# Loading wq by two issues of 16 and 112 partitions in a one-core decode kernel

## The chip, the cores and the metric

The kernel runs on one core of a Trainium2 chip. The metric is the time of one execution on the device, in microseconds; a kernel's time is the median of its runs. The core has five engines that run side by side, each with its own list of instructions: TensorE (PE in the profile; PEld are its weight loads), VectorE (DVE), ScalarE (ACT), GpSimd (POOL) and SyncE (SP), which here does nothing but issue transfers. Transfers between the device's main memory and the core's on-chip memory are carried by 16 DMA engines. The on-chip memory has 128 partitions; a tile of 128 rows has one row in each.

## What is computed

One decode step: attention over a cache of 4096 keys and values for each of 32 heads, a small MLP, and a gate that mixes the two.

```
B, Sq, D = 1, 1, 512;  Hq = Hkv = 32;  Sk, Dh = 4096, 128;  F = 1376      # all bf16
q = (x @ wq).reshape(B, Sq, Hq, Dh).transpose(0, 2, 1, 3)
scores = einsum("bhqd,bhkd->bhqk", q, k_cache) * Dh ** -0.5
o = einsum("bhqk,bhkd->bhqd", softmax(scores), v_cache)
a = o.transpose(0, 2, 1, 3).reshape(B, Sq, Hq * Dh) @ wo
r = relu(x @ w1 + b1);  b = (r * r) @ w2 + b2
g = sigmoid((x * gate_w).sum(-1))
out = g * a + (1 - g) * b
```

The caches are 32 MB each, wq and wo 4 MB each, w1 and w2 1.4 MB each.

## The kernel before

The 32 heads are taken in eight groups of four (NQ = 8, R = 4). A group's keys are one tile of 128 partitions by 32 KB, four heads of 32 partitions each, and so are its values; K and V have two slots each in the tile KV, used in turn. The query weights are one tile W of the same shape: wq is viewed as 128 rows of four consecutive input rows each (line 75), so that each partition takes 32 KB. Later the same tile W takes wo.

Every large transfer is issued by SyncE, in one queue. The first is wq (line 235), ahead of the block in which the engines' own lists begin. Then `load_kv` goes through ORDER (line 60): K0 K1 V0 K2 V1 K3 and so on to V7. A load into a slot that was used before waits for the group that had it (`done`, line 255: for K, VectorE's sums and TensorE's transposes; for V, the products with the values). In between, w1 and b1 go out after the sixth load, the larger part of wo after the fourteenth, the rest of wo at the end, and last the four pieces of w2, when VectorE is done with the tile `prod` that shares their place. One of these pieces, w2b (line 267), has 96 rows; wq, K, V, w1, wo and the other pieces of w2 have 128. ScalarE issues three small loads (x, gate_w, b2) in its own queue at the start.

Each transfer adds 16 to a semaphore when all of it is in place: `s_wq` for wq, `s_k[q]` and `s_v[q]` for the caches, and so on.

The work at the start goes in this order. TensorE turns x into columns (line 575); VectorE spreads each column over a tile xb (line 655) and takes the gate's sum (line 659, `s_zp`). TensorE waits for wq (line 577) and for `s_zp`, then runs `q_rows` for four groups of heads (line 437: four matmuls of 512 columns for a group); ScalarE copies each group's query into the rows of qb (line 339); `q_cols` turns these into columns (line 444). The other four groups follow inside the first two rounds of the main loop. Of each group's keys, three eighths are multiplied with the query and summed on VectorE (lines 685 and 689), and the rest transposed by TensorE (line 453), copied by ScalarE (line 356), and multiplied by TensorE (line 460). The softmax and the products with the values (line 495) follow; the outputs go through wo, the MLP is added, and 1 KB is written out.

The two waits that the text speaks of stand in TensorE's list as

```
eng.wait_ge(s_wq, 16)
eng.wait_ge(s_zp, 1)
for c in range(QF):
    q_rows(c)
```

## Time and profile before

| | |
|---|---|
| median of 3 runs | 190.35 us (190.35 to 190.43) |
| profiled execution | 190.46 us, of which the span of the trace is 189.1 us |
| busy, share of the span | PE 73%, PEld 61%, DVE 66%, ACT 61%, POOL 1% |
| moved | 78.46 MB in 3648 packets, mean 415 GB/s |
| K loads, issue to landing | 19.9 us (median of 8) |
| V loads, issue to landing | 25.6 us (median of 7) |
| wq, issue to landing | 12.4 us |

The span begins with the first instruction in the trace and ends with the last. Busy shares are means over the span. An issue's time to landing runs from the issuing instruction to the full count of its semaphore, so it holds what was queued ahead of it. A packet is one contiguous piece that one DMA engine carries.

### The profile page before, as it was taken

What the parts mean: (1) busy time and instruction counts of PE and PEld (TensorE: products, weight loads), DVE (VectorE), ACT (ScalarE), POOL (GpSimd) and SP (SyncE); (2) the same over time, 40 slices, a digit from 0 to 9 for tenths busy, and PEclk for the clock granted to TensorE, in tenths of its full rate; (3) what the DMA queues carried; (4) which work ended last, traced back from release to release, by engine and by line L of the source; (5) the groups of instructions that cost most, each with busy time, mean ns of one, the idle gap of its engine ahead of it and who ended that gap; (6) DMA issues with size and microseconds to landing.
All of it is one profiled execution on the core that took longest, in us unless ns stands there. A gap on an engine that the chain in (4) does not pass through costs nothing. (4 is left out here: it accounts for less than half of the span.)

```text
span 189.1 us, 5915 instructions
## 1 busy us (share of the span) xinstructions
PE 137.8 (73%) x2553; PEld 115.9 (61%) x2553; DVE 125.6 (66%) x134; ACT 115.0 (61%) x237; POOL 2.6 (1%) x13
## 2 busy tenths in 40 slices
PE   0029398496615967496998899799969968798683
PEld 0003276375515857495996799599859857338682
DVE  1110299999979946995899999669964998202020
ACT  3006499759972985198689809976984985500000
POOL 5000000000000000000000000000000000000000
PEclk9999969969955995588559657955985996589555
DMA  6999999999999999999999999999999999999991
GB/s 222 444 444 444 444 444 426 395 418 433 437 433 444 433 395 463 423 433 409 423 430 445 423 437 437 444 437 423 416 423 437 435 423 447 437 411 421 412 389 65
DMA packets 3648, 78.46 MB, mean 415 GB/s; under 512 B 468, under 2 KB 694, under 8 KB 950
## 3 DMA queue, kind: packets, MB, share of 16 engines
q1 hardware_dynamic: 3626, 78.32, 97.1%
q8 instruction: 6, 0.10, 0.2%
q14 instruction: 4, 0.03, 0.0%
q10 hardware_dynamic: 12, 0.00, 0.0%
HBM read 78.32 MB, written 0.00 MB: 414 GB/s over the span
## 5 line engine op out<-in xcount | busy, mean ns | idle before, releaser
L356 ACT ACTIVATE kT<-KP 128x1024 bf16<-128x1024 bf16 x80 | 75.1, 1047 | 24.9 <-PE KP L453 24.7
L685 DVE TENSOR_TENSOR w2a<-KV,qb 128x1536 f32<-128x1536 bf16 x32 | 56.0, 1751 | 6.9 <-DMA KV<-in_A_k_cache_dram 6.4
L453 PE MATMUL KP<-ident,KV 128*128 128x128 bf16 x640 | 58.2, 251 | 1.6 <-PEq L448 1.6
L689 DVE TENSOR_REDUCE S<-w2a 128x12 f32<-128x1536 f32 x32 | 56.1, 1753 | 1.1
L453 PEld LDWEIGHTS KP<-ident,KV 128*128 128x128 bf16 x640 | 47.4, 114 | 4.6 <-issue 3.5
L460 PE MATMUL pS<-qc,kT 128*128 128x4 bf16 x640 | 28.0, 165 | 13.6 <-PEq L448 11.1
L460 PEld LDWEIGHTS pS<-qc,kT 128*128 128x128 bf16 x640 | 24.3, 99 | 20.0 <-issue 18.8
L495 PEld LDWEIGHTS pO<-E,KV 128*128 128x128 bf16 x1024 | 28.6, 103 | 2.4 <-issue 2.3
L495 PE MATMUL pO<-E,KV 128*128 128x4 bf16 x1024 | 28.3, 166 | 2.2 <-PEq L448 2.2
L373 ACT ACTIVATE E<-S,nM 32x128 bf16<-32x128 f32 x32 | 18.6, 581 | 0.9
L437 PE MATMUL pQ<-W,xb 128*128 128x512 bf16 x20 | 7.1, 492 | 5.6 <-DMA W<-in_A_wq_dram 4.8
L481 PE MATMUL pM<-identf,mp 128*1 128x128 f32 x8 | 3.0, 371 | 11.1 <-PEq L448 11.1
L362 ACT ACTIVATE S<-pS 32x80 f32<-32x80 f32 x32 | 7.3, 229 | 4.8 <-PE pS L460 4.2
L339 ACT ACTIVATE qb<-pQ 32x128 bf16<-32x128 f32 x20 | 5.4, 269 | 7.4 <-PE pQ L437 7.0
L694 DVE TENSOR_REDUCE mp<-S 128x1 f32<-128x128 f32 x8 | 2.3, 286 | 10.7 <-ACT S L362 10.6
L708 DVE RECIPROCAL rden<-pO 128x4 f32<-128x4 f32 x8 | 1.4, 174 | 10.4 <-PE pO L495 10.4
L373 ACT ACTIVATION_READ_ACCUMULATOR E<-S,nM 32x1 f32 x32 | 8.1, 254 | 0.0
L535 PE MATMUL KP<-W,o 128*1 128x512 bf16 x24 | 7.7, 496 | 0.4 <-PEq L448 0.4
L481 PEld LDWEIGHTS pM<-identf,mp 128*1 128x1 f32 x8 | 0.6, 80 | 11.4 <-issue 11.2
L664 DVE TENSOR_SCALAR e<-ez 128x1 f32<-128x1 f32 x1 | 0.2, 154 | 9.8 <-ACT ez L382 9.8
L437 PEld LDWEIGHTS pQ<-W,xb 128*128 128x128 bf16 x20 | 1.9, 114 | 7.7 <-DMA W<-in_A_wq_dram 4.8
L575 PE MATMUL pO<-ident,w_sb 1*128 1x1 bf16 x4 | 0.3, 164 | 8.2 <-DMA w_sb<-in_A_x_dram 8.2
(81 smaller groups left out, 66.5 us busy)
## 6 DMA issues: line engine op xcount, KB each, us to landing
KV<-in_A_k_cache_dram SPq DMA_DIRECT2D x8, 4096.0 KB, 19.9
KV<-in_A_v_cache_dram SPq DMA_DIRECT2D x7, 4096.0 KB, 25.6
W<-in_A_wq_dram SPq DMA_DIRECT2D x1, 4096.0 KB, 12.4
W<-in_A_wo_dram SPq DMA_DIRECT2D x1, 3072.0 KB, 33.1
KV<-in_A_v_cache_dram SPq DMA_DIRECT2D x1, 3072.0 KB, 18.3
w_sb<-in_B_w_dram SPq DMA_DIRECT2D x1, 1376.0 KB
KV<-in_A_v_cache_dram SPq DMA_DIRECT2D x1, 1024.0 KB, 20.5
W<-in_A_wo_dram SPq DMA_DIRECT2D x1, 1024.0 KB, 22.5
```

The costliest lines, as they stand in the source:

```text
L339: eng.activation(qb[rows(r), c, :], QR[c][rows(r), r * 128:(r + 1) * 128], ACT.Copy)\
L356: eng.activation(kT[:, n % NT, :], KP[n % NKP][:, :], ACT.Copy).then_inc(s_ev, 1)
L362: eng.activation(S[rows(r), q % NS, 0:YQ], S2[rows(r), :, r], ACT.Copy).then_inc(s_cp, 1)
L373: eng.activation(E[rows(r), q % 2, :, r], S[rows(r), q % NS, :], ACT.Exp, bias=nM[rows(r), q:q + 1], scale=SCALE, accum_out=RS[rows(r), q ...
L437: mm = eng.matmul(QR[c], xb[:, t, :], wq_sb[:, t, c * 512:(c + 1) * 512], start=(t == 0), stop=(t == 3))
L453: mm = eng.transpose(KP[(GQ * a + g) % NKP][:, y * 128:(y + 1) * 128], key(a, b), ident[:, :])
L460: mm = eng.matmul(pS[:, R * c:R * c + R], kT[:, (GQ * a + g) % NT, y * 128:(y + 1) * 128], qc2[:, a, :], start=True, stop=True)
L481: eng.transpose(MT, mp[:, a:a + 1], identf[:, :]).then_inc(s_mt, 1)
L495: mm = eng.matmul(O[a], KV[:, V_SLOT[a], b * 128:(b + 1) * 128], E[:, a, COLUMN[b], :], start=(b == 0), stop=(b == NB - 1))
L535: mm = eng.matmul(RA, o2[:, t:t + 1], wo_sb[:, t, :], start=(t == 0), stop=(t == TA - 1))
L685: eng.tensor_tensor(prod, KV[:, K_SLOT[q], x:x + XB * 128].rearrange("p (b d) -> p b d", d=128), qb[:, q, :].unsqueeze(1).to_broadcast([12 ...
L689: eng.tensor_reduce(S[:, q % NS, c:c + XB], prod, AX.X, ALU.add).then_inc(s_sd, 1)
```

## The change

wq is no longer loaded by one issue of 128 rows, but by two on the same queue: first partitions 0 to 15, then partitions 16 to 127. Both add 16 to the same semaphore, and TensorE waits for 32 instead of 16. All else is as before.

```
-        nc.sync.dma_start(W[:, :], wq_v).then_inc(s_wq, 16)
+        for p, e in ((0, 16), (16, 128)):
+            nc.sync.dma_start(W[p:e, :], wq_v[p:e, :]).then_inc(s_wq, 16)
...
-            eng.wait_ge(s_wq, 16)
+            eng.wait_ge(s_wq, 32)
```

## The prediction

> **What bounds the kernel now.** I read the slices of the span first, for what is busy from end to end; then the chain of waits, for what ends last; then the timeline of the start, around the changed line; then the windows over the end, the one place where a load of other than 128 full rows of partitions runs beside others.

> From the page (slices, queues, chain):

> ```profile
> DMA  6999999999999999999999999999999999999991
> GB/s 222 444 444 444 444 444 426 395 418 433 437 433 444 433 395 463 423 433 409 423 430 445 423 437 437 444 437 423 416 423 437 435 423 447 437 411 421 412 389 65
> ...
> q1 hardware_dynamic: 3626, 78.32, 97.1%
> ...
> DMA w2a<-in_B_w_dram 13%; PE pO L495 2%; SPq L252 0%; PE pQ L560 0%; SPq L265 0%; SPq L280 0%; PE pO L490 0%; PE pO L641 0%; DVE fin L767 0%; DVE accs L765 0%
> ```

> The 16 DMA engines are nine tenths busy or more in 38 of the 40 slices, and one queue, SyncE's, carries 78.32 MB and takes 97.1% of their time. No other engine is near that (PE 73%, DVE 66%, ACT 61%). The chain of waits ends with the w2 loads: they land 24.7 us after their issue because everything issued before them is still being carried. So the time is: when the stream starts, plus the bytes at the stream's rate, plus 2.7 us of work after the last landing (186.4 to 189.1). A microsecond lost by the slowest DMA engine anywhere is a microsecond at the end, as nothing later in the stream stands idle to take it up. Arithmetic that is merely late costs nothing unless it makes an issue come too late for the queue, which holds 20 us and more (the median K load lands 19.9 us after its issue, V 25.6).

> The start, from the timeline:

> ```profile
> 0.74 0.38 SPq L235 DMA_DIRECT2D W<-in_A_wq_dram  x1
> ...
> 1.17 0.89 SPq L247 DMA_DIRECT2D KV<-in_A_k_cache_dram  x2
> ...
> 13.16 0.13 PEld L437 LDWEIGHTS pQ<-W,xb 128*128 128x128 bf16 x2 [4.83 <-DMA W<-in_A_wq_dram]
> ...
> 22.74 1.76 DVE L685 TENSOR_TENSOR w2a<-KV,qb 128x1536 f32<-128x1536 bf16 x1 [1.04 <-DMA KV<-in_A_k_cache_dram]
> ```

> One issue costs SyncE 0.38 us, the first packet starts at 1.84 us, wq is there at 13.1 and K0 at 22.7: 9.6 us for each 4 MB.

> Windows over the steady stream and over the end (columns: stretch, length, busy time and count of PE, PEld, DVE, ACT, POOL, granted clock, DMA share, GB/s):

> ```profile
> 110.00:160.00 50.00, 44.12 (x964) 40.58 (x961) 41.63 (x40) 38.64 (x71) 0.00 (x0) 0.74 1.00 431
> 160.00:183.00 23.00, 18.93 (x304) 13.15 (x303) 3.46 (x15) 2.48 (x9) 0.00 (x0) 0.65 0.99 422
> 183.00:184.00 1.00, 0.65 (x24) 0.64 (x24) 0.45 (x3) 0.00 (x0) 0.00 (x0) 0.50 1.01 383
> 184.00:184.50 0.50, 0.38 (x15) 0.30 (x12) 0.00 (x0) 0.00 (x0) 0.00 (x0) 0.50 0.85 229
> 185.50:186.00 0.50, 0.50 (x21) 0.50 (x22) 0.00 (x0) 0.00 (x0) 0.00 (x0) 0.50 0.44 154
> ```

> GB/s divided by 16 times the share is the rate of a busy DMA engine: 422 / (16 x 0.99) = 26.6 in the steady stream, but 229 / (16 x 0.85) = 16.8 at 184.0 to 184.5, and 154 / (16 x 0.44) = 21.9 again at the very end. At 184 the engines are busy and yet slow. The DMA packets recorded in the trace, sorted by size, say which:

> ```
> packets of    count  shortest  median  longest (ns)
> 32768 B       2048     1211     1213     2171   all over 1300: the first 16, and 10 beside code loads
>  6144 B        128      234      239      364
>  3072 B        128      121      124      220
>  1024 B        224       46       46       93
> ```

> A 32 KB row takes 1213 ns on every engine, with 16 of them running, for 160 us: in a load of 128 rows the engines don't touch each other. The long 6144, 3072 and 1024 byte packets all lie between 183.6 and 184.8 us, while w2b (L267, 96 rows, six for each engine) passes. So a load whose rows do not come to 128 sends engines to places in the on-chip memory where they stand in each other's way, and slows also the engines that still carry a 128-row load.

> **The change part by part.** (1) One issue more on SyncE: +0.38 us, by L235. It moves the K0, K1, V0 issues back by as much; K0's packets start 9.7 us after wq's, so it is hidden; were that cover gone it would cost 0.38. (2) One completion packet more on each DMA engine: in the trace these 4-byte packets take 9 ns, so 0.01 us. (3) The bytes are the same: 16 rows are one for each of 16 engines and 112 are seven, together the eight that each had (w2b's even six per engine speaks for the even split). (4) The start of the stream: its first packet could come earlier, as fewer rows are described in the first issue. The trace doesn't show how its 1.84 us depends on the rows; the bounds are nothing and a gain of 7/8 of the 0.38 us issue, 0.33. I take 0. (5) TensorE's wait for wq, now for both loads: behind it stand the q_rows matmuls, ScalarE's copies, q_cols, the first transposes of K0, and VectorE's first product, which waits for the copies. They take from 13.2 to 21.5 us, less than the 9.6 us between the landings of wq and K0; so they move with wq, K0 still comes last, and no term of its own arises. x and gate_w (8.1 and 10.6 us) wait behind wq's packets and get later by some microseconds too, but are needed with wq, not before it.

> (6) What decides: wq's eight rows per engine, 8 x 1.213 = 9.70 us, now come in two loads neither of which has 128 rows. The trace shows no such load of 32 KB rows; w2b is the nearest row. Below: nothing collides, +0. Next: 26.6 / 16.3, where 16.3 is the lowest rate in the windows of 0.2 us (184.2 to 184.4: 282 / (16 x 1.08)), a factor of 1.63: +6.1 us. Above: the worst single packet, 93 / 46 = 2.02: +9.9 us. The first understates, since at 184 a part of the engines still carried well-placed rows, and here all 16 start odd loads within 0.8 us of each other; the second is the worst of 224. Between these two I take the middle, +8.0. From that comes something off: only the DMA engine that is last at the end counts. The 16 engines now end between 184.1 and 186.4 us, in two clumps, so that the engine losing most in wq need not be the one that is last now. I take off a third of that spread, 0.7.

> [...]

> Sum against the profiled run: 190.46 + 0 + 0.01 + 0 + 8.0 - 0.7 = 197.8; the runs' median lies 0.11 lower, so **197.7 us**.

> **The rivals.** (A) Only the 16-row load collides; the 112 rows are dealt so that every engine keeps mostly to its place. [...] For it: 112 is nearer to 128; against: w2b's 96 rows did collide. Chance 0.10. (B) The engines take every sixteenth row of the 112, so that all 16 sit on 16 neighbouring rows in all eight rounds. [...] Chance 0.05. (C) The other side: nothing collides with 32 KB rows, because the slowing at 184 belongs to short packets, and the first issue, with an eighth of the rows, sets the stream going earlier, up to 0.33 us, all of which arrives at the end: 190.0. It decides from the point where the collisions cost less than what the start gains. For it: the stream has no idle stretch to swallow a gain. Against: 6144-byte packets were slowed by half. Chance 0.06. (D) Nothing collides and the start depends on the first row alone: 190.4, the two small terms being hidden. Chance 0.07.

> **How the numbers follow.** My forecast has 0.72. Its own range is +6.1 to +9.9 on 190.35 with the spread taken off or not: 195.7 to 200.3. To hold 8 in 10 the range reaches down into A, where it holds most of that case, to 192.0, and up by one more packet and the exposed issue, 1.2 + 0.4, to 202.0; B, C and D, 0.18, stay out. A measurement of this kernel can tell 0.2% (0.4 us) from no change. C is mostly faster by less than that: of its 0.06 I count 0.03 as faster, and 0.02 more for an order of engines that happens to shorten the end; same is the other 0.03 of C with D less that 0.02, 0.08; slower 0.87.

> **What would show it.** In the changed profile the two loads at the head of SyncE's queue land together at about 21 us and not at 13.1; the GB/s of the slices of the first 20 us fall well below 444 while the DMA share stays at nine tenths; K0's first product starts at about 30 us; from there all loads run at the old rate, and the tail after the last landing stays 2.7 us. The packets of wq last well over 1213 ns, those of K1 and later 1213 again. The prediction is wrong if wq's packets keep 1213 ns, or if wq lands late and the end does not move, which would mean that the stream has slack that the slices hide.

## The result, and the profile after

The changed kernel takes 199.63 us (median of 6 runs, 199.25 to 199.76), the kernel before 190.42 us (190.35 to 190.64) on the same chips: a ratio of 1.0478, 95% interval 1.0465 to 1.0492. The change costs 9.2 us. The profiled execution took 199.70 us, of which the span is 198.3.

From the page of the changed kernel, the slices and the chain of waits:

```profile
DMA  7998999999999999999999999999999999999991
GB/s 106 211 318 212 397 423 430 430 420 423 425 426 430 420 433 419 465 417 420 430 423 436 423 431 436 436 443 430 436 430 423 430 420 430 434 438 413 408 392 61
...
DMA w2a<-in_B_w_dram 12%; PE pO L497 2%; SPq L254 0%; PE pQ L562 0%; SPq L267 0%; SPq L282 0%; PE pO L492 0%; PE pS L462 0%; PE pM L487 0%; PE pO L643 0%; DVE fin L769 0%; DVE accs L767 0%
```

In the first four slices (20 us) the DMA engines are about as busy as before (0.7, 0.9, 0.9 and 0.8; before 0.6 and three times 0.9), but they carry 106, 211, 318 and 212 GB/s where they carried 222 and then 444. From the sixth slice on the rate is about the old one. The chain ends with the same w2 load. So the engines are busy and slow in the first 20 us, and nothing later takes it up.

The timeline of the start (start, duration, what; the line numbers are two higher than before):

```profile
0.74 0.85 SPq L237 DMA_DIRECT2D W<-in_A_wq_dram  x2
...
17.25 0.68 DVE L661 CUSTOM_DVE_ANT_0 w_sb<-w_sb 1x512 bf16<-1x512 bf16 x1 [2.83 <-DMA w_sb<-in_gate_w_dram]
...
22.57 0.13 PEld L439 LDWEIGHTS pQ<-W,xb 128*128 128x128 bf16 x2 [9.31 <-DMA W<-in_A_wq_dram]
...
32.30 1.76 DVE L687 TENSOR_TENSOR w2a<-KV,qb 128x1536 f32<-128x1536 bf16 x1 [0.66 <-DMA KV<-in_A_k_cache_dram]
```

wq is there at 22.6 us instead of 13.2, K0 at 32.3 instead of 22.7: 9.4 and 9.6 us later. The gate's sum, delayed from 10.6 to 17.3 us, still comes before wq, so that TensorE does not wait for it.

The end of the chain in order of time (start, duration, what), first of the kernel before, then of the changed one:

```profile
161.71 24.68 DMA w2a<-in_B_w_dram
186.38 0.04 issue
186.43 0.71 PE pQ L560 x20
```

```profile
172.07 23.49 DMA w2a<-in_B_w_dram
195.56 0.05 issue
195.61 0.76 PE pQ L562 x20
```

The last landing (start plus duration of the DMA line) moved from 186.39 to 195.56 us, by 9.2 us, which is the whole loss; after it come 2.7 us as before. The packets of the first nine rows that each DMA engine carries, sorted by their start into rounds of 16 (nearly one for each engine), say where the time lies:

```
mean duration of a round's 16 packets of 32 KB, us
round            1     2     3     4     5     6     7     8   | K0's first
before         1.86  1.22  1.21  1.21  1.21  1.21  1.21  1.21 |  1.21
after          3.58  2.86  2.29  1.83  1.79  1.99  2.26  2.15 |  1.79
```

Round 1 of the changed kernel is the load of 16 partitions, rounds 2 to 8 the load of 112. The first eight rounds sum to 18.74 us after and 10.35 before: 8.39 us, of which 1.72 fall to the 16 rows and 6.67 to the 112. Another 0.57 us fall to K0's first row, which sets off while the last of the 112 are still under way. That makes 8.96 of the 9.2. Over the whole stream the packets of SyncE's queue take 192.65 us per DMA engine in the mean instead of 183.55: the mean engine loses 9.1 us, and the end moves by 9.2.

### The profile page after: what moved, and what is told of

Same layout as the page of the kernel before. It is cut to its first block, busy times and chain, and to the rows that moved or that the text cites. A ratio compares the mean times of both kernels' runs of the same rounds, so it can differ in the third digit from the quotient of the medians.

```text
span 198.3 us, 5916 instructions
## 1 busy us (share of the span) xinstructions
PE 139.2 (70%) x2553; PEld 116.7 (59%) x2553; DVE 125.4 (63%) x134; ACT 115.0 (58%) x237; POOL 2.6 (1%) x13
## 3 DMA queue, kind: packets, MB, share of 16 engines
q1 hardware_dynamic: 3642, 78.32, 97.1%
HBM read 78.32 MB, written 0.00 MB: 395 GB/s over the span
## 5 line engine op out<-in xcount | busy, mean ns | idle before, releaser
L455 PE MATMUL KP<-ident,KV 128*128 128x128 bf16 x640 | 59.6, 255 | 1.2 <-PEq L450 1.2
L455 PEld LDWEIGHTS KP<-ident,KV 128*128 128x128 bf16 x640 | 48.6, 116 | 4.1 <-issue 3.1
L439 PE MATMUL pQ<-W,xb 128*128 128x512 bf16 x20 | 7.8, 531 | 10.1 <-DMA W<-in_A_wq_dram 9.2
L577 PE MATMUL pO<-ident,w_sb 1*128 1x1 bf16 x4 | 0.3, 165 | 13.1 <-DMA w_sb<-in_A_x_dram 13.1
L666 DVE TENSOR_SCALAR e<-ez 128x1 f32<-128x1 f32 x1 | 0.2, 154 | 13.2 <-ACT ez L384 13.2
L577 PEld LDWEIGHTS pO<-ident,w_sb 1*128 1x128 bf16 x4 | 0.2, 109 | 13.1 <-issue 13.1
L657 DVE TENSOR_SCALAR xb<-zeros,xcolf 128x128 bf16<-128x128 bf16 x4 | 0.7, 248 | 11.2 <-ACT xcolf L334 11.2
## 6 DMA issues: line engine op xcount, KB each, us to landing
KV<-in_A_v_cache_dram SPq DMA_DIRECT2D x1, 3072.0 KB, 17.3
W<-in_A_wo_dram SPq DMA_DIRECT2D x1, 1024.0 KB, 21.5
```

Of the source, the lines that this page charges most:

```text
L439: mm = eng.matmul(QR[c], xb[:, t, :], wq_sb[:, t, c * 512:(c + 1) * 512], start=(t == 0), stop=(t == 3))
L455: mm = eng.transpose(KP[(GQ * a + g) % NKP][:, y * 128:(y + 1) * 128], key(a, b), ident[:, :])
```

## The experiments

**Reading against writing.** Four kernels load wq by eight issues of 16 rows, with near (neighbouring) or far (every eighth) rows on either side.

```
-        for p, e in ((0, 16), (16, 128)):
-            nc.sync.dma_start(W[p:e, :], wq_v[p:e, :]).then_inc(s_wq, 16)
+        for r in range(8):                       # near write, near read
+            nc.sync.dma_start(W[16*r:16*r+16, :], wq_v[16*r:16*r+16, :]).then_inc(s_wq, 16)
...
+            nc.sync.dma_start(W[r:128:8, :], wq_v[r:128:8, :]).then_inc(s_wq, 16)          # far, far
...
+            nc.sync.dma_start(W[r:128:8, :], wq_v[16*r:16*r+16, :]).then_inc(s_wq, 16)     # far write
...
+            nc.sync.dma_start(W[16*r:16*r+16, :], wq_v[r:128:8, :]).then_inc(s_wq, 16)     # far read
...
-            eng.wait_ge(s_wq, 32)
+            eng.wait_ge(s_wq, 128)
```

> wq comes by eight issues of 16 rows, each from 16 neighbouring rows of memory into 16 neighbouring partitions. Theory L (the engines collide where neighbouring partitions are written) and theory S (they collide where neighbouring rows are read) both expect it slow: 199 to 200 us if the 112-row load of the changed kernel already went round by round over 16 neighbouring rows, about 204 if that load gave each engine a block of seven (eight rounds at the 2.9 us of the first two instead of 1.21). Theory B (a short load is slow by itself) expects about 204 as well.

> Eight issues of 16 rows; issue r takes every eighth row of memory into every eighth partition. L and S expect it faster than the near kernel, 190.4 to 196 us; B expects the same as the near kernel.

> Eight issues of 16 rows; issue r reads 16 neighbouring rows of memory and writes every eighth partition (so the rows of the query weights stand in other partitions than their inputs, and the query is another one). L expects the time of the kernel that is far on both sides, 190.4 to 196 us; S expects that of the near kernel, 199 to 204; B the same as the near kernel.

> Eight issues of 16 rows; issue r reads every eighth row of memory and writes 16 neighbouring partitions (the query is again another one). L expects the time of the near kernel, 199 to 204 us; S expects that of the kernel far on both sides, 190.4 to 196; B the same as the near kernel.

Measured: near and near 216.62 us, far and far 201.16, far write alone 200.72, far read alone 216.88. The write side sets the time; the read side changes it by 0.3 to 0.4 us, which single executions can't tell from nothing. S and B fall. All four numbers lie above what I had expected: I had put "eight rounds at 2.9 us" where the rounds are longer still. The windows of DMA share and GB/s show it (stretch, length, granted clock, share, GB/s; a packet counts whole in the window in which it starts, so that a share can come out above 1); first near and near, then far write, then the kernel before:

```profile
6.00:20.00 14.00, 1.00 1.04 120
```

```profile
6.00:20.00 14.00, 1.00 1.08 225
```

```profile
6.00:20.00 14.00, 1.00 1.04 447
```

Near writing runs at about a quarter of the rate of the kernel before, far writing at half. In packets: from the second round on, near rounds take 4.52 us each, 3.7 times 1.213; far ones take 2.55 us, 2.1 times (one of the eight 2.36).

**How the 112 rows are dealt, and whether another cut does as much.** One kernel imitates the load of 112 rows by seven issues that give each engine a block of seven neighbours, one after the other; the others cut wq into halves, cut it by columns, or leave wq whole and cut K3.

```
+        nc.sync.dma_start(W[0:16, :], wq_v[0:16, :]).then_inc(s_wq, 16)                     # blocks
+        for i in range(7):
+            nc.sync.dma_start(W[16 + i:128:7, :], wq_v[16 + i:128:7, :]).then_inc(s_wq, 16)
...
+        for p, e in ((0, 64), (64, 128)):                                                   # halves
...
+        for p, e in ((0, 2048), (2048, 16384)):                                             # columns
+            nc.sync.dma_start(W[:, p:e], wq_v[:, p:e]).then_inc(s_wq, 16)
...
+                    for p, e in ((0, 16), (16, 128)) if q == 3 else ((0, 128),):            # K3
+                        eng.dma_start(KV[p:e, K_SLOT[q], :], k_q[q, p:e, :]).then_inc(s_k[q], 16)
```

> The first 16 rows as in the change; the other 112 by seven issues, issue i taking row 16 + i and every seventh row after it, so that each DMA engine is given, one by one, a block of seven neighbouring partitions. If the 112-row load of the changed kernel deals its rows in such blocks, the packets come out as there (rounds of about 2.9, 2.3, 1.8, 1.8, 2.0, 2.3, 2.2 us) and the time is 199 to 200.5 us. If it deals them otherwise, the time is off by more than 1 us, either way; with 16 neighbouring rows in each round it would be 215 us or more.

> wq by two issues of 64 partitions each, four rows for each engine. [...] With 16 neighbouring rows in each round: 216 us. Theory that it is the odd count of 16 and 112 that hurts: 190.4.

> wq by two issues as in the change, but cut by columns: first 4 KB of each of the 128 rows, then the other 28 KB; TensorE waits for both. L: no engine leaves its path, so 190.0 to 190.8 us. Theory that the second issue or the second completion costs: 199 us.

> wq by one issue as before; instead K3, the sixth load of the main stream, is split into 16 and 112 partitions, and its readers wait for both. If the loss is in the DMA engines' busy time and the stream has no slack anywhere, it is the same loss less the start of the first packet: 198 to 200 us. If the loss has to do with the start (TensorE waiting for wq with nothing else to do), 190.4 to 192.

Blocks: 199.44 us, as forecast, with rounds of 3.65, 2.79, 2.20, 1.86, 1.70, 1.95, 2.22, 2.12 us, those of the changed kernel within 0.1 us each. So the load of 112 rows most likely deals each engine a block of seven neighbouring partitions. Halves: 201.08 us, rounds of 2.56 us, as with every eighth partition (2.55): the cut of 16 and 112 is not special, and an even one costs more. Columns: 190.46 us beside 190.59; the second issue, the second completion and the wait for both cost nothing that a single execution can tell, with all 128 partitions in each load.

K3: 204.47 us, a loss of 13.9, more than I had expected. From its page:

```profile
DMA  7999999999997998899999999999999999999980
GB/s 277 446 413 413 413 465 448 426 415 410 452 448 129 203 271 181 274 444 419 452 439 426 421 426 432 439 439 426 432 413 452 439 415 434 424 432 418 408 319 17
```

The dip from 444 to between 129 and 274 GB/s has moved to slices 13 to 17 (61 to 86 us), where K3 passes. That the loss belongs to the load and not to the start is shown. Why it is 4.7 us larger than for wq is shown only in part. The engines set off on K3's 112 rows 2.4 us apart (63.3 to 65.7 us; on wq's 112 rows 0.5 us), rounds 2 to 8 take 2.2 to 2.7 us, 16.9 in sum (wq's 1.8 to 2.9, 15.2 in sum), and behind them w1's 11 KB packets take 513 ns in the median instead of 418. Of the 14.0 us by which the stream got longer, 12.2 are busy time of the DMA engines; the other 1.8 are idle time. SyncE waited 20.6 us instead of 9.3 in total for VectorE to free the K slots; that this made the idle time is argued. That the larger spacing of the engines makes the collisions last longer is argued, not tested.

**Why every engine is slow.** In rounds 4 and 5 of the changed kernel, the two shortest of the eight (1.83 and 1.79 us in the mean), three quarters of the packets lie between 1.69 and 1.81 us, and none is faster, where a 32 KB row in a load of 128 rows takes 1.21. Theory P says that only the engines that collide are slow; X, that their collision holds up the others too; N, that an engine which writes other partitions than in a full load is slow even alone. The last four kernels leave wq whole and send three more loads of 16 rows behind it, into slots of KV that are overwritten later. K1's issue waits until they have landed. The four patterns of partitions were chosen to have no pair of colliding engines (twice), one pair and two pairs, and the runs are named for it; which partitions make a pair, and which ones an engine writes in a full load, was the author's assumption, and no run shows it.

```
         nc.sync.dma_start(W[:, :], wq_v).then_inc(s_wq, 16)
+        for c in range(1, 4):
+            nc.sync.dma_start(KV[16:122:7, c, :], wq_v[16:122:7, :]).then_inc(s_ex, 16)
...
+                if n == 1:
+                    eng.wait_ge(s_ex, 48)
```

The partitions above, 16:122:7, are those meant to have two pairs; the others are 32:93:4 (no pair, the engines' own partitions), 11:117:7 (no pair, other partitions) and 28:89:4 (one pair).

> wq by one issue as before; behind it three more loads of 16 rows each (partitions 32, 36, ... 92) into slots of KV that are overwritten later, so three more packets of 32 KB for each DMA engine and nothing else. [...] All theories in which a short load is harmless by itself: packets of 1213 ns, 190.5 + 3 x 1.21 = 194.1 us. If a load of 16 rows is slow whatever it writes: 195.5 us or more.

> [...]

> [...] Theory P: two packets of each round of 16 take about 2.5 us and the other 14 take 1213 ns; the end is 194.1 us if the two engines are not those that end last, up to 198.0 if they are. [...] N: as P but more packets slow.

> [...] P: four packets of a round at about 2.5 us, twelve at 1213 ns, 194.1 to 198.0 us. X: all 16 packets slow, 1.7 to 2.3 us as in the rounds of the changed kernel, 195.6 to 197.5 us. [...]

Measured: 193.99 us with 32:93:4, 194.63 with 11:117:7, 198.28 with 28:89:4 and 198.08 with 16:122:7. The windows over the extra loads (columns as above, and rough, since so short a window holds few packets), in the order 32:93:4, 11:117:7, 28:89:4 and 16:122:7:

```profile
13.00:16.00 3.00, 1.00 1.07 459
```

```profile
13.00:16.00 3.00, 1.00 0.90 382
```

```profile
13.00:16.00 3.00, 1.00 0.85 328
```

```profile
13.00:16.00 3.00, 1.00 0.85 175
```

```
packets of the three extra rounds, ns
                 1st round        2nd round              3rd round
32:93:4          1213 all         1213 all               1213 all
11:117:7         1218 to 1285     1213 to 1224           1213 to 1220
28:89:4          1405 to 1488,    1256 to 1320,          1219 to 1295,
                 1844, 1995       2508, 2585             1761, 3034
16:122:7         1538 to 2080     2520 to 2529, all 16   2519 to 2586, all 16
```

With the first two patterns a load of 16 rows is as fast as one of 128 or nearly so, 1213 ns for every row with 32:93:4 and 1213 to 1285 with 11:117:7: nothing speaks for N (of the 0.64 us by which the second of these runs is longer, 0.16 lie in K0's first packets, 1.36 to 1.46 us, at the change-over, and the rest in the start and along the stream, which single executions can't tell from their spread). With 16:122:7 all 16 engines run at 2.52 us in the second and third round, 2.1 times 1.213. P's forecast for it, four slow packets and twelve at 1213 ns, did not come, and X's, all 16 slow, did; that most of the 16 only share in a hold-up by two pairs rests on the assumed pairs and is not shown. The partitions of 28:89:4 are those of 32:93:4 but for one, 28 in place of 92, and here two packets in each round stand out (1844 and 1995, 2508 and 2585, 1761 and 3034 ns), as many as one pair would make. The effect on the other 14 is there but small, 0.5 to 23% in these rounds, where X would have all 16 slow; K0's first two rounds then take 1.5 to 1.8 us on most engines. 28:89:4 costs as much time as 16:122:7 all the same, 4.3 and 4.1 us beside the run with 32:93:4: with 28:89:4 the mean engine is busy for 2.8 us more and the last landing moves by 4.3, since the slowest engines set the end; with 16:122:7 the figures are 4.0 and 4.1, since all lose alike. Why 16:122:7 slows all engines alike and 28:89:4 mostly two, the runs don't show.

No version beats the kernel before: the one cut that cost nothing, by columns, gained nothing that a single execution can tell.

## Why the prediction was right

By its own steps. **(1), (2)** The second issue (0.85 us for both instead of 0.38) and the second completion are hidden, as the cut by columns shows; the completion packets of the 16 rows take 35 ns, not 9, which is as little. **(3)** The rows are split evenly, one and seven for each engine, as the blocks kernel bears out. **(4)** The first packet starts in the same window as before, at 1.75 to 2.00 us; the term of 0 was right for it. The last of the 16 engines does set off 0.5 us earlier (at 2.10 instead of 2.61 us; the mean engine 0.14), so a small part of the gain of rival C exists; it is gone in the first collision. **(5)** TensorE's wait moved with wq, and K0 still comes last, 9.7 us after it.

**(6)** The term that decides was right in kind and nearly in size: a mean factor of 1.81 over the eight rows against the 1.82 that lies in the middle of my two rows, 8.39 us against 8.0. That the middle came so near is in part luck: the two rows were read from packets of 1 to 6 KB, and from round to round the factor goes from 1.5 to 2.35, beyond the 2.02 that I had taken as the upper end. The reading behind the term was also too wide. It is not rows short of 128 in themselves that put engines in each other's way, since the 16 rows of 32:93:4 took 1213 ns each; it is the partitions that the 16 engines write together: a round took 2.52 us with 16:122:7, 2.55 with every eighth partition and 4.52 with 16 neighbours.

The 1.9 us between forecast (197.7) and time (199.6) come from three places in the main. The deduction of 0.7 us, "only the DMA engine that is last at the end counts", should not have been made: the mean engine loses 9.1 us, and the one that ends last, at 9.2, loses no less. K0's first row, 0.57 us, was not in the sum. The remaining 0.4 are in what the factor applies to: I had put all eight rows at 1.213 us, 9.70 in sum, but the first one takes 1.86 already in the kernel before, and the eight 10.35. These make 1.7; another 0.2 was not followed further.

No run shows the 192.0 that the range owes to rival A: in the changed kernel the 16 rows cost 1.7 us, and the 112 rows another 6.7. The round of the 16 rows took 3.58 us, and near rounds later in a stream 4.52; why the first one is shorter stays open.

**The rivals.** A fell: the 112 rows cost 6.67 of the 8.39 us. B fell: blocks of seven gave the rounds of the changed kernel within 0.1 us each, while eight rounds on 16 neighbouring partitions, as B has them, took 216.6 us. C and D fell with the collisions.

Of the signs that I named, all but one came: wq at 22.6 us (I had said about 21), K0's first product at 32.3 (about 30), a busy share of 0.7 to 0.9 at half the rate, about 1213 ns again from K0's second row on (1216 in the median), and 2.7 us after the last landing. One I had wrong: the two loads do not land together; the 16 rows land at 7.3 us, the 112 at 22.5.

## What to carry to other kernels

A stream of loads that keeps the DMA engines busy has one number to watch, the rate of a busy engine (GB/s over 16 times the share): in the windows of the first experiments it was 26.9 in the kernel before and 7.2 with near writing, at the same share of 1.04, and the engines were in each other's way. Cut such a load by columns, not by partitions: all 128 partitions in each piece cost nothing here, while 16 and 112 cost 9.2 us and 64 and 64 cost 10.5 for the same 4 MB. A short load is not slow in itself: 16 rows four partitions apart (32, 36, ... 92) ran at the full 1213 ns for a row, though the same spacing from 28 to 88 cost 4.3 us more. What such a cut lost here didn't hide behind a deep queue; it came out at the end in full.

## What was not expected of the hardware

Sixteen rows at the partitions 16, 23, ... 121 slow all 16 engines to 2.52 us for a 32 KB row, as much as every eighth partition does (2.55), while 16 rows at 11, 18, ... 116, just as far apart, take 1213 to 1285 ns. And where the rows come from made no difference that single executions can tell: 16 neighbouring rows of the main memory or every eighth, 256 KB apart, differ by 0.4 us at most over 4 MB.
